# Filling expert buckets from both ends, and loading an expert's weights and a row block earlier, in a fused attention and mixture-of-experts kernel

## The chip, the cores and the metric

The kernel runs on one core of one Trainium2 chip. The metric is the device time of one execution in microseconds (us). Executions of one kernel on one chip mostly agree within about 1.5% (run 6 below spreads by 2.3%). The same kernel on different chips does not: the kernel before took about 524 us on two of the chips used here, and about 547 us on the chip of run 12 and on that of the first timed runs (the record gives no number for the latter; it may be the same chip). Every comparison below is between runs on the same chip.

## The reference, cut to what matters

Attention over 8 batches, 8 heads, 576 positions, head size 64, causal by blocks of 64. Its output, 4608 tokens of 512 numbers, goes through a router that picks two of eight experts for each token, and each expert is a two-layer network.

```python
logits = x @ w_gate
noisy_logits = logits + np.log1p(np.exp(x @ w_noise)) * noise
top2 = np.argpartition(-noisy_logits, 2, axis=1)[:, :2]
...                                   # softmax over the two: top2_w
for e in range(8):
    for k in range(2):
        mask = top2[:, k] == e
        h = np.maximum(x[mask] @ w1[e], 0.0)              # 512 -> 1024
        out[mask] += top2_w[mask, k, None] * (h @ w2[e])  # 1024 -> 512
```

## The kernel before

Attention runs in four groups of nine row tiles (128 tokens each). After each group a router on VectorE finds each token's two experts and its two slots, and 18 indirect transfers scatter the rows into `xd`, a buffer in device memory with eight buckets of `CAP` = 640 rows for each half of the tokens. The second half of the kernel works on 16 blocks, each one expert for one half: four experts of half 0, the same four of half 1, then experts 4 to 7 in turn for both halves.

A block's rows come by a transposing load from the SyncE queue (SP). Weights come by the GpSimd queue. A token's two experts are added by way of memory: the lower-numbered expert stores its weighted result to `yd` (`ysb`), the higher-numbered one gathers it (`yg`), adds it (`yo`) and scatters the sum to the output. Before the change a bucket mixes both kinds of rows, so every tile of experts 1 to 6 does both.

```python
def load_x(b):                                   # SP: one transposing load
    half, e = SEQ[b]
    xg = ffn["x"].tile([P, DB, CAP], BF16, tag="xg", name="xg")   # two buffers
    ins = nc.sync.dma_start_transpose(out=xg, in_=xd[half][e * CAP:(e + 1) * CAP, 0:Dm])
    for nm in scat[half]:                        # waits for all scatters of its half
        tc.add_manual_dep(ins.ins, nm, SYNC_DEP, reason="rows landed")
    xgs[b] = xg

def load_w(pool, e):                             # GpSimd: w1, then w2
    ...

def layer2(b, c):
    ...                                          # eight matmuls into yp
    if e + 1 < E:
        ysb = ffn["y"].tile([P, Dm], BF16, tag="ysb", bufs=4)
        nc.scalar.activation(out=ysb, in_=yp, func=AF.Copy, scale=w)
        nc.sync.dma_start(out=yd[half][e * CAP + c * P:e * CAP + (c + 1) * P, :], in_=ysb)
    if e:
        yo = ffn["y"].tile([P, Dm], F32, tag="yo", bufs=4)
        nc.vector.scalar_tensor_tensor(out=yo, in0=yp, scalar=w, in1=ygs.pop((b, c)),
                                       op0=ALU.mult, op1=ALU.add)
        ins = nc.gpsimd.indirect_dma_start(out=out, ...)          # by trow
```

The loop over the steps of the second half issues the loads. `at(slot, ...)` runs a job at the end of the same step.

```python
for b in range(NB):
    steps += [(layer1, b, fb) for fb in range(0 if b == 0 else 1, FB)]
    if b + 1 < NB:
        steps.append((layer1, b + 1, 0))
    steps += [(layer2, b, c) for c in range(CT)]
...
for fn, b, j in steps:
    fn(b, j)
    if fn is layer1 and j == FB - 1:
        if b + 2 < NB:
            if b + 2 == 4:
                at(slot, load_rec, 1)
                at(slot + 12, read_rec, 1)
            at(slot, load_x, b + 2)
        if b in (3, 7):
            at(slot, load_w, wL, 4 + (b - 3) // 4)
        if b in (5, 9):
            at(slot, load_w, wE, 6 + (b - 5) // 4)
    if fn is layer1 and SEQ[b][1] and j in GJ:
        gather(b, GJ.index(j))
    run(slot)
```

The softmax here doesn't subtract the row's maximum and nothing guards it: scores larger than these inputs give would overflow.

Of the kernel before, what the change touches and what calls it, by code (L numbers as in the profile page):

```python
# [8 lines left out]
F32 = mybir.dt.float32  # L9
BF16 = mybir.dt.bfloat16  # L10
# [9 lines left out]
def kernel(  # L20
# [23 lines left out]
    TG = 9  # L44
# [11 lines left out]
    ZR = 512  # L56
# [49 lines left out]
    qk_pool = right.enter_context(tc.tile_pool(name="qk", bufs=1, side="right"))  # L106
# [9 lines left out]
    ecend = consts.tile([P, E, 1], F32)  # L116
    ecap_i = consts.tile([P, E, 1], I32)
    rmask = consts.tile([P, E, TG], F32)
    ovrow_i = consts.tile([P, 2, TH], I32)
    ovrow = consts.tile([P, 2, TH], F32)  # L120
    base = [consts.tile([P, E, 1], F32, name=f"base{i}") for i in range(NH)]
# [11 lines left out]
    def setup_consts():  # L133
        nc.vector.memset(ones_mat, 1.0)
        nc.vector.memset(rmask, 1.0)
        nc.vector.memset(rmask[:, :, 0:1], 0.0)
# [23 lines left out]
        for i in range(NH):  # L160
            nc.vector.tensor_copy(base[i], ecap_i)
        nc.vector.tensor_copy(ebeg, ecap_i)
        nc.vector.tensor_scalar(ecend, ecap_i, float(CAP), None, op0=ALU.add)
# [9 lines left out]
    qT = qk_pool.tile([P, 73 * 64], BF16)  # L173
    kT = qk_pool.tile([P, 73 * 64], BF16)
    anchors = {}
    pace = {}
# [75 lines left out]
    def score_unit(g, u):  # L252
# [32 lines left out]
        pace["last"] = ins.ins.name  # L285
# [52 lines left out]
    def router(g):  # L338
        half, t0 = g // 2, g * TG
        lg = av_ps.tile([P, TG, 2 * E], F32, tag="av")  # L340
        for idx in range(TG):
            for db in range(DB):
# [26 lines left out]
        m = rt.tile([P, E, TG], BF16, tag="m")  # L369
        nc.vector.tensor_add(m, oh[:, 0], oh[:, 1])  # L370
# [4 lines left out]
        mf = m.rearrange("p e t -> p (e t)")  # L375
        pp = av_ps.tile([P, 2, E * TG], F32, tag="av")
# [3 lines left out]
        incl = rt.tile([P, E, TG], F32, tag="incl")  # L380
        nc.vector.tensor_tensor_scan(out=incl.rearrange("p e t -> p (e t)"),
                                     data0=rmask.rearrange("p e t -> p (e t)"),
                                     data1=pp[:, 0, :], initial=0.0, op0=ALU.mult, op1=ALU.add)
        pos = rt.tile([P, E, TG], F32, tag="pos")
        nc.vector.tensor_tensor(out=pos.rearrange("p e t -> p (e t)"),
                                in0=incl.rearrange("p e t -> p (e t)"), in1=pp[:, 1, :], op=ALU.add)
        yield
        nc.vector.tensor_tensor(out=pos, in0=pos, in1=base[half].to_broadcast([P, E, TG]), op=ALU.add)
        nc.vector.tensor_tensor(out=base[half], in0=base[half], in1=incl[:, :, TG - 1:TG], op=ALU.add)
        yield  # L390
        ov = rt.tile([P, E, TG], F32, tag="ov")
        nc.vector.tensor_tensor(out=ov, in0=pos, in1=ecend.to_broadcast([P, E, TG]), op=ALU.is_ge)
        nc.vector.scalar_tensor_tensor(out=pos, in0=ov, scalar=BIG, in1=pos, op0=ALU.mult, op1=ALU.add)
        yield
        sl2 = rt.tile([P, 2, TG], F32, tag="sl2")
        pk = rt.tile([P, 2, E, TG], F32, tag="pk")
        nc.vector.tensor_tensor(out=pk, in0=oh, in1=pos.unsqueeze(1).to_broadcast([P, 2, E, TG]),
# [30 lines left out]
    def scatter(g, j):  # L428
# [7 lines left out]
        tc.add_manual_dep(ins.ins, pace["last"], SYNC_DEP, reason="spreads the descriptors over time")  # L436
# [27 lines left out]
    def read_rec(half):  # L464
# [22 lines left out]
        nc.vector.tensor_tensor(out=fill, in0=rowid, in1=base[half].to_broadcast([P, E, CT]), op=ALU.is_lt)  # L487
# [10 lines left out]
    def layer1(b, fb):  # L498
        half, e = SEQ[b]
        w1sb = wload[e][0]  # L500
        if fb == 0:
            hs[b] = ffn["h"].tile([P, FB, CAP], BF16, tag="hsb", name="hsb")
# [8 lines left out]
        pace["last"] = ins.ins.name  # L511

    def layer2(b, c):
# [11 lines left out]
        if e:  # L525
# [14 lines left out]
    def gather(b, c):  # L540
# [10 lines left out]
        tc.add_manual_dep(ins.ins, pace["last"], SYNC_DEP, reason="spreads the descriptors over time")  # L551
# [23 lines left out]
    def clear_x(half, slot):  # L575

        for e in range(E):
            n = CAP - ZR
            ins = nc.sync.dma_start(out=xd[half][e * CAP + ZR:(e + 1) * CAP, :], in_=zero[0:n, 0:DR])
            after(ins, slot)  # L580
# [8 lines left out]
    def flags():  # L589
        nc.vector.tensor_tensor(out=fl, in0=base[0], in1=ecend, op=ALU.subtract)  # L590
        nc.vector.tensor_tensor(out=fl2, in0=base[1], in1=ecend, op=ALU.subtract)
        nc.vector.tensor_tensor(out=fl, in0=fl, in1=fl2, op=ALU.max)
        nc.vector.reduce_max(flm, fl[:, :, 0], axis=AX.X)
        nc.vector.tensor_scalar(flag_i, flm, 0.0, None, op0=ALU.is_gt)
# [4 lines left out]
    fl = keep.tile([P, E, 1], F32)  # L599
    fl2 = keep.tile([P, E, 1], F32)  # L600
# [67 lines left out]
    at(2 * UG + 22, load_w, wE, 0)  # L668
    at(3 * UG + 12, load_w, wE, 1)
    for u in range(NG * UG):  # L670
        score_unit(*divmod(u, UG))
        run(u)
        if u == 3 * UG + 18:
            raws_up.close()
            ffn["x"] = raws_up.enter_context(tc.tile_pool(name="xgp", bufs=2, side="right", reuse_waits="tile"))
            ffn["h"] = raws_up.enter_context(tc.tile_pool(name="hp", bufs=2, side="right", reuse_waits="tile"))
            load_x(0)
            load_rec(0)
            load_x(1)

# [13 lines left out]
    wL = None  # L694
    for fn, b, j in steps:
        fn(b, j)
        if fn is layer1 and j == FB - 1:
            if b + 2 < NB:
                if b + 2 == 4:
                    at(slot, load_rec, 1)  # L700
                    at(slot + 12, read_rec, 1)
                at(slot, load_x, b + 2)
            if b in (3, 7):
                at(slot, load_w, wL, 4 + (b - 3) // 4)
            if b in (5, 9):
                at(slot, load_w, wE, 6 + (b - 5) // 4)
        if fn is layer1 and SEQ[b][1] and j in GJ:
            gather(b, GJ.index(j))
        run(slot)
        slot += 1  # L710
        if slot == NG * UG + 6:
            top.close()
            wL = top.enter_context(tc.tile_pool(name="wL", bufs=3, reuse_waits="tile"))
# [92 lines left out]
```

## Time and profile before

| | us |
|---|---|
| timed runs, before the prediction (3) | 548.15 median, 546.17 to 548.84 |
| profiled run | 525.0, span 523.2 |
| granted TensorE clock in the profile | 0.885 |

The timed runs and the profile differ by 4.4%. The lines of the profile that carry the argument are shown and read in the prediction. In short: the expert stage is bound by TensorE (PE), with stretches in which PE stands idle, called holes here. Most of them lie in its first third, where weights, row loads and indirect transfers share the DMA engines. Two more words: a transfer is *issued* by an engine's queue (SP or GpSimd, in traces POOL) and *lands* when its last bytes have arrived.

### The profile page before, as it was taken

The page shows a single profiled execution, that of the slowest core. Times are in us where ns is not written, and L with a number is a line of the kernel's source. Part 1 is how long each engine was busy: PE and PEld are TensorE (multiplying, and loading weights), DVE is VectorE, ACT ScalarE, POOL GpSimd, SP SyncE. Part 2 cuts the span into 40 slices and gives each one's busy share as a digit, 9 for nine tenths or more (in the row PEclk, how much of TensorE's full clock was granted, in tenths as well). Part 3 has the DMA queues.
Part 4 walks back from the last instruction along what each step waited for, and adds up shares of the span by engine and source line. Part 5 has one row for each costly group of instructions (what it writes and reads, how often), then busy time and mean ns, then how long its engine had stood idle before and what let it go on. Part 6 is the DMA issues. An engine that isn't in the chain of part 4 may idle for free.

```text
span 523.2 us, 10093 instructions
## 1 busy us (share of the span) xinstructions
PE 424.6 (81%) x3944; PEld 257.6 (49%) x3944; DVE 182.5 (35%) x482; ACT 238.3 (46%) x319; POOL 294.5 (56%) x331
## 2 busy tenths in 40 slices
PE   2787978978871992596559999799699799999991
PEld 2455655745650751353235665465355455565550
DVE  4275797797880460020221102112122022112211
ACT  0856766767760240344114554454344434555230
POOL 9675285797571353387745225375276365565561
PEclk9957996998975896699669999999889989999997
DMA  8999799399779699661266929729939935645331
GB/s 133 146 145 214 110 183 208 116 127 187 186 145 187 92 170 221 161 163 66 67 144 129 233 64 193 165 79 201 196 116 186 239 123 169 156 145 183 122 103 50
DMA packets 142743, 78.77 MB, mean 151 GB/s; under 512 B 102931, under 2 KB 131754, under 8 KB 142688
## 3 DMA queue, kind: packets, MB, share of 16 engines
q0 software_dynamic: 73376, 55.87, 64.4%
q1 hardware_dynamic: 69312, 22.19, 20.8%
q8 instruction: 33, 0.54, 0.4%
q14 instruction: 22, 0.18, 0.1%
HBM read 71.43 MB, written 39.42 MB: 212 GB/s over the span
## 4 chain that ended last, share of the span: by engine, by line
PE 37%; DMA 18%; issue 16%; POOL 14%; DVE 6%; ACT 4%; SPq 2%; POOLq 1%; DVEq 0%; ACTq 0%
PE hp L506 14%; PE yp L518 13%; DMA yd<-ysb 7%; POOL out_dram L529 5%; POOL yg L547 4%; PE sc L266 3%; DMA xd<-xr,slots 3%; DMA t<-in_k_dram 3%; PE av L303 2%; ACT esc L269 2%; PE tp L228 2%; POOL xd L431 2%; DMA vt<-in_v_dram 2%; DMA t<-in_q_dram 2%; SPq L585 2%
## 5 line engine op out<-in xcount | busy, mean ns | idle before, releaser
L506 PE MATMUL hp<-xg,w1sb 128*128 128x320 bf16 x1024 | 149.5, 307 | 33.9 <-ACT hsb L509 22.3
L518 PE MATMUL yp<-w2sb,hsb 128*128 128x512 bf16 x640 | 149.0, 391 | 20.8 <-DVE yo L527 20.1
L527 DVE SCALAR_TENSOR_TENSOR yo<-yp,wrow,yg 128x512 f32<-128x512 f32 x70 | 52.5, 750 | 263.5 <-ACT ysb L523 155.3
L506 PEld LDWEIGHTS <-w1sb 128*128 128x128 bf16 x1024 | 102.3, 100 | 79.1 <-issue 34.8
L509 ACT ACTIVATE hsb<-hp 128x640 bf16<-128x640 f32 x128 | 89.8, 704 | 82.5 <-PE hp L506 82.5
L529 POOL DMA_INDIRECT out_dram<-yo,trow x70 | 69.6, 994 | 87.2 <-DVE yo L527 62.9
L269 ACT ACTIVATE esc<-sc 128x1024 bf16<-128x1024 f32 x96 | 94.4, 1029 | 52.1 <-PE sc L266 49.8
L518 PEld LDWEIGHTS <-hsb 128*128 128x128 bf16 x640 | 64.0, 100 | 100.4 <-issue 34.1
L523 ACT ACTIVATE ysb<-yp,wrow 128x512 bf16<-128x512 f32 x70 | 48.1, 687 | 127.9 <-PE yp L518 96.9
L431 POOL DMA_INDIRECT xd<-xr,slots x72 | 71.6, 994 | 58.0 <-ACT hsb L509 29.5
L547 POOL DMA_INDIRECT yg<-yd,orow x70 | 71.0, 1014 | 38.6 <-ACT hsb L509 22.1
L266 PE MATMUL sc<-qT,kT 64*128 64x512 bf16 (+4 forms) x320 | 43.8, 340 | 9.3 <-ACT esc L269 7.9
L195 POOL DMA_DIRECT2D vt<-in_v_dram x40 | 33.7, 879 | 14.7 <-PE av L314 10.0
L303 PE MATMUL av<-vt,esc 128*128 128x65 bf16 x640 | 35.6, 212 | 5.5 <-DVE xr L318 5.1
L303 PEld LDWEIGHTS <-esc 128*128 128x128 bf16 x640 | 27.9, 109 | 18.3 <-DVE xr L318 8.9
L228 PE MATMUL tp<-ident,t 128*64 128x128 bf16 x512 | 26.8, 268 | 6.1 <-DVE qT L233 3.7
L318 DVE TENSOR_TENSOR xr<-av,rden 128x256 bf16<-128x256 f32 x72 | 30.5, 424 | 2.6
L228 PEld LDWEIGHTS <-t 128*64 128x64 bf16 x512 | 21.5, 139 | 14.1 <-issue 6.2
L235 DVE COPY kT<-tp 128x1024 bf16<-128x1024 bf16 (+1 forms) x24 | 25.0, 1042 | 4.7 <-PE tp L228 4.2
L317 DVE RECIPROCAL rden<-av 128x4 f32<-128x4 f32 x72 | 13.0, 181 | 27.8 <-PE av L303 18.9
L266 PEld LDWEIGHTS <-kT 64*128 64x128 bf16 x320 | 11.5, 97 | 18.7 <-issue 11.7
L233 DVE COPY qT<-tp 128x1024 bf16<-128x1024 bf16 (+1 forms) x24 | 14.7, 612 | 16.7 <-PE tp L228 16.5
(110 smaller groups left out, 193.3 us busy)
## 6 DMA issues: line engine op xcount, KB each, us to landing
yd<-ysb SPq DMA_DIRECT2D x70, 128.0 KB
w1sb<-in_moe_w_dram POOLq DMA_DIRECT2D x8, 1024.0 KB
w2sb<-in_moe_w_dram POOLq DMA_DIRECT2D x8, 1024.0 KB
t<-in_q_dram POOLq DMA_DIRECT2D x16, 256.0 KB
t<-in_k_dram POOLq DMA_DIRECT2D x16, 256.0 KB
vt<-in_v_dram POOLq DMA_DIRECT2D x32, 128.0 KB
xd<-zero SPq DMA_DIRECT2D x16, 132.0 KB
nz_all<-in_moe_noise_dram SPq DMA_DIRECT2D x72, 2.0 KB
```

The lines of the kernel that those rows point to most:

```text
L228: nc.tensor.transpose(to[64 * hf:64 * hf + 64, :, r, :], raw[:, hf, r * 64:(r + 1) * 64], ident)
L266: nc.tensor.matmul(out=sc[:, hf, off:off + z - a], lhsT=kT[sl, c0 + jt * P:c0 + jt * P + P], rhs=qT[sl, c0 + a:c0 + z], start=True, stop=True)
L269: ins = nc.scalar.activation(out=esc[:, hh, :, piece * 512:(piece + 1) * 512], in_=sc, func=AF.Exp, scale=scale)
L303: nc.tensor.matmul(out=av[:, hh, :], lhsT=esc[:, hh, hf, c:c + P], rhs=vb[:, 4 * hf + jt, h, :], start=(jt == 0), stop=(jt == ib))
L431: ins = nc.gpsimd.indirect_dma_start(out=xd[half].bitcast(I32), out_offset=bass.IndirectOffsetOnAxis(ap=slots[:, g * TG + idx, i:i + 1], a ...
L506: nc.tensor.matmul(out=hp[:, n, 0:NW], lhsT=w1sb[:, db, fb * P:(fb + 1) * P], rhs=xgs[b][:, db, n * NW:(n + 1) * NW], start=(db == 0), sto ...
L509: ins = nc.scalar.activation(out=hs[b][:, fb, :].rearrange("p (n w) -> p n w", n=2), in_=hp[:, :, 0:NW], func=AF.Relu)
L518: nc.tensor.matmul(out=yp, lhsT=hs[b][:, fb, c * P:(c + 1) * P], rhs=w2sb[:, fb, :], start=(fb == 0), stop=(fb == FB - 1))
L523: nc.scalar.activation(out=ysb, in_=yp, func=AF.Copy, scale=w)
L527: nc.vector.scalar_tensor_tensor(out=yo, in0=yp, scalar=w, in1=ygs.pop((b, c)), op0=ALU.mult, op1=ALU.add)
L529: ins = nc.gpsimd.indirect_dma_start(out=out, out_offset=bass.IndirectOffsetOnAxis(ap=trow[half][:, e, c:c + 1], axis=0), in_=yo, in_offse ...
L547: ins = nc.gpsimd.indirect_dma_start(out=yg, out_offset=None, in_=yd[half][0:e * CAP, :], in_offset=bass.IndirectOffsetOnAxis(ap=orows[hal ...
```

## The change

It has two parts, and they serve one aim, which is to empty the holes.

**Buckets.** Rows whose expert is the token's first (lower-numbered) one fill their bucket from the top; rows whose expert is the second fill it from the bottom. Then only the lower row tiles of a bucket, `LT` of them, gather and write the output: 46 of each in place of 70. The router pays for it with seven more VectorE instructions for each group and doubled sizes of some others.

**Loads.** The weights of expert 2 and row block 2 come in the last attention group. Row loads move forward by some steps. The weights of experts 4 to 7 get new places: those of expert 5 move forward by four steps, those of experts 4, 6 and 7 back by one and a half to three and a half blocks. Now three of the four stand at step 3. Queries, keys and the hidden rows of layer 1 share one tile, `hq`.

```diff
+    LT = (0, 1, 2, 3, 3, 4, 5, 5)
...
+        c2 = rt.tile([P, TG, E], F32, tag="c2")          # running count in a token's row
+        nc.vector.tensor_tensor_scan(out=c2.rearrange("p t e -> p (t e)"), ...)
+        ms = rt.tile([P, 2, E, TG], BF16, tag="ms")      # [0]: minus first expert, [1]: second
+        nc.vector.scalar_tensor_tensor(out=msv[1], in0=c2, scalar=2.0, in1=m, op0=ALU.is_equal, op1=ALU.mult)
+        nc.vector.tensor_tensor(out=msv[0], in0=msv[1], in1=m, op=ALU.subtract)
... (positions, limits and choice of slot for both ends)
-        if e:
+        if c < LT[e]:
             yo = ffn["y"].tile([P, Dm], F32, tag="yo", bufs=4)
...
-    at(2 * UG + 22, load_w, wE, 0)
-    at(3 * UG + 12, load_w, wE, 1)
+    at(2 * UG + 24, load_w, wE, 0)
+    at(3 * UG + 15, load_w, wE, 1)
...
-            ffn["x"] = raws_up.enter_context(tc.tile_pool(name="xgp", bufs=2, ...))
+            ffn["x"] = raws_up.enter_context(tc.tile_pool(name="xgp", bufs=3, ...))
+            wM = raws_up.enter_context(tc.tile_pool(name="wM", bufs=1, ...))
             load_x(0)
             load_rec(0)
             load_x(1)
+            load_x(2)
+            load_w(wM, 2)
...
-        if fn is layer1 and j == FB - 1:
-            ... (row load b + 2, then weights, as above)
+        if fn is layer1:
+            if j == 0 and b and b + 2 < NB and b + 2 != 4:
+                load_x(b + 2)
+            if (b, j) == (3, 4):
+                load_rec(1)
+                load_x(4)
+            if (b, j) == (4, 3):
+                read_rec(1)
+            if (b, j) in WL:
+                load_w(*WL[b, j])
+            if j in GJ and GJ.index(j) < LT[SEQ[b][1]]:
+                gather(b, GJ.index(j))
...
+            WL = {(5, 7): (wE, 4), (7, 3): (wE, 5), (9, 3): (wM, 6), (11, 3): (wL, 7)}
```

Indirect transfers also wait for the activation before the last now (`pace[-2]`), not the last. The middle of each bucket, where valid rows may be missing, is cleared in 16 pieces of 96 rows for each half in place of eight of 128.

## The prediction

> **What bounds the kernel now.** I read the slices of the page first, for where TensorE (PE) is not busy, then the costliest groups, for what a block of the second half costs, then the chain of waits and the timeline, for what each hole waited for.
>
> The slices of the page, each 13.08 us of the 523.2:
>
> ```profile
> PE   2787978978871992596559999799699799999991
> DVE  4275797797880460020221102112122022112211
> PEclk9957996998975896699669999999889989999997
> ```
>
> Attention ends near 157 us, in slice 12 (counted from 0), where PE falls to 1. The expert stage runs from there. It is at 9 nearly throughout once past 270 us, but slices 15, 16, 18, 19 and 20 show 2, 5, 6, 5, 5. So the second half is bound by PE, with large holes in its first third. DVE matters in attention only.
>
> From the costliest groups: duration sums, mean ns of one, idle before:
>
> ```profile
> L506 PE MATMUL hp<-xg,w1sb 128*128 128x320 bf16 x1024 | 149.5, 307 | 33.9 <-ACT hsb L509 22.3
> L518 PE MATMUL yp<-w2sb,hsb 128*128 128x512 bf16 x640 | 149.0, 391 | 20.8 <-DVE yo L527 20.1
> L529 POOL DMA_INDIRECT out_dram<-yo,trow x70 | 69.6, 994 | 87.2 <-DVE yo L527 62.9
> L547 POOL DMA_INDIRECT yg<-yd,orow x70 | 71.0, 1014 | 38.6 <-ACT hsb L509 22.1
> ```
>
> 16 blocks (one expert of one half of the tokens) each have 64 matmuls of layer 1 and 40 of layer 2. In the chain, undisturbed, layer 1 of a block takes 8.69 us and layer 2 8.72 us: 17.4 us a block, 278.6 us for 16. PE really ends at about 511.7, 342.3 us after the stage starts at 169.4. About 11 us of that are the rest of the last attention group and its router. So some 52 us are holes and the slow clock after them. That is what can be won here.
>
> The chain of waits, start and duration in us, around the change of stage and in the first block:
>
> ```profile
> 151.20 12.51 DMA xd<-xr,slots
> 163.83 5.52 DMA xg<-xd
> 169.39 2.29 PE hp L506 x8
> ...
> 199.10 1.19 SPq L450
> 200.39 13.07 DMA yd<-ysb
> 213.57 0.70 ACT ysb L523
> ```
>
> The timeline has the holes themselves; the bracket is idle time and releaser:
>
> ```profile
> 186.29 14.01 SPq L450 DMA_TRANSPOSE xg<-xd  x1
> ...
> 214.90 8.37 PE L506 MATMUL hp<-xg,w1sb 128*128 128x320 bf16 x48 [15.81 <-ACT hsb L509]
> ...
> 222.22 2.50 SPq L450 DMA_TRANSPOSE xg<-xd  x1
> ...
> 253.82 8.05 PE L518 MATMUL yp<-w2sb,hsb 128*128 128x512 bf16 x24 [9.68 <-DVE yo L527]
> ...
> 270.39 9.61 PE L506 MATMUL hp<-xg,w1sb 128*128 128x320 bf16 x48 [6.35 <-ACT hsb L509]
> ```
>
> Hole A, 157.9 to 169.4: the last scatter of half 0 takes 12.5 us to land, because expert 1's weights were issued just ahead of it (147.68 and 148.48); then the first transposing load takes 5.5. Hole B, 15.8 us: the load of row block 2 needs 14.01 us to issue on the SP queue beside the weights of expert 2 (from 182.3); the ysb stores stand behind it in that queue and need 13 us more beside expert 3's weights; there are four ysb buffers, so the fifth ysb of block 0 waits, and ScalarE (ACT) with it. Hole C, 9.7 us: GpSimd (POOL) issues an indirect transfer every 1.3 us from about 229 to 258 (18 scatters of the last group, gathers and output scatters in between); the gather for yo comes late. Hole D, 6.35 us: row block 4 waits for the last half-1 scatter (issued 257.1), and again stores stand behind the transpose. Hole E, 2.8 to 3.0 us each or in pairs near 339, 374, 379 and 418, 10.6 in sum: the fifth yo waits for a buffer whose output scatter is behind a weight load, so POOL is late with the next gathers.
>
> **What the Trainium skill says.** "DMA: Bandwidth & Descriptors", section "Queues, rings and completion order": each DMA engine takes the rows it has work for in turn, a packet at a time, and data of one ring is consumed in ring order. The trace agrees: a scatter behind weights took 12.5 us against 2.46 for one with none before it (at 239.63), and a transpose from SP beside weights took 14.01 us against 2.50. The same page, "Issuing engines are not separate DMA queues", says that all queues share 16 engines; so moving the weights earlier only moves the contention. "TensorE: Matmul & The Clock Gate", section "Part 1: The HAM clock gate", has the clock fall to half after an idle of about 3.4 us. The trace agrees: after hole C 24 matmuls took 8.05 us, 335 ns each, against 218.
>
> **The change part by part.** (1) Rows whose expert is the token's first are filled from the top, the others from the bottom; only bottom tiles gather and write the output. The limits (0,1,2,3,3,4,5,5) add to 23, so 46 gathers and 46 output scatters replace 70 of each. 48 POOL issues of 1.3 us go: 62 us of POOL, none directly on PE's path but in C and E. 24 DVE yo of 0.75 us go as well (18 us, DVE idle there). The valid rows moved stay the same. I counted the reference's routing for this draw: at most 361 rows for the 384 of expert 4, 416 of 512 for expert 5, 580 of 640, and 624 of 640 in a bucket, so the slow fallback is not taken.
>
> Between 200 and 262 blocks 1 to 3 need 2, 4 and 6 indirect transfers in place of 10 each: 18 x 1.3 = 23 us less POOL beside the 18 remaining scatters. C should vanish: 9.7 us, and 2.8 of slow clock (24 x (335-218) ns): 12.5. E should mostly go: blocks of experts 4 and 5 have 3 and 4 yo tiles for four buffers, and the last weights are issued in block 11, before those of five tiles. 10.6 plus 3 of clock, less 3 that I leave: 10.6.
>
> (2) Loads. Expert 2's weights and row block 2 now come in the last attention group; one expert instead of two is loaded from block 0 on. In A, expert 1's weights follow the last scatter. It is issued at 151.2 - 1.2 (it now waits for the activation before the last) - 1.8 (two weight issues no longer ahead) + 4.5 (DVE, below) = 152.7 and lands 3 us later, 155.7, not 163.7. But the transpose now runs beside 8.4 MB of weights, at 14 to 15 us as at 186.29, not 5.5: rows come at about 170.5. So A is a wash, +1. In B, SP has four transposes in a row beside weights; experts 1 to 3 (12.6 MB at about 270 GB/s, 8.4 MB in the 31 us from 182.3 to 213.6) end near 202 rather than 214. The first stores then go at about 205 and land 3 us later. PE resumes at 209 instead of 214.9: 6 us won.
>
> (3) Row block 4 and the records of half 1 are issued in block 3, at layer 1 step 4, only four steps (4 x 1.09 = 4.4 us) before they are needed; records (about 3 us, from 5.44 against 2.5 for the transpose behind them at 260.24) and load (5.5) take 8.5. D becomes a wait of 4 us plus 1.5 of clock in place of 6.35 plus 3.1: 4 us won.
>
> (4) The router has seven more DVE instructions and larger ones. By its own rows: a scan 0.29, three strided writes (0.28 more for one, 0.48 for two; line 360's is 0.48), one more comparison 0.23, three for the choice 0.69, doubled sizes 0.3: 2.8 us a group. In attention DVE is at 12.0 of 13 us in the stretch from 65 to 78, so I let 80% of three groups count: 6 us later at the end of attention, 4.5 of it ahead of half 0's last scatter (in A already). The fourth runs under the experts. Clearing 16 pieces in place of 8 per half adds SP issues of 0.6 us that nothing waits for.
>
> **Sum.** PE resumes after B at 209. From there 117 steps of layer 1 (1.088) and 75 of layer 2 (1.744) remain: 258 us. Add 5.5 for row block 4, 2 for a late half-1 scatter (the next load waits for it on SP), 3 for what stays of E: 477.5. The tail behind the last matmul (511.7 to 523.2, 11.5) stays: 489. The timed runs are longer than the profiled one by 548.15/523.2; 489 x 1.0477 = 512.
>
> **The rivals.** First, A gets worse: the first transpose shares the engines with two experts' weights throughout, and takes longer than 14 us since 18 scatters of group 2 are in the rings too. For it: the 14.01. Against: at 186.29 there were six scatters as well. If the start slips 8 us and B does not shrink, 489 becomes 503, or 527 timed. Second, the SP queue is the bound in B: four transposes at 14 us from 155.7 end at 212, and B stays whole, only C to E are won: 495, 519 timed. Third, better than I think: transposes are as quick as 5.5 us, so PE starts when attention does end, at 164, and B vanishes (resuming at 195): 475, 498 timed. For it: the transpose at 369.48 took 5.45 with a weight load nearly done. Fourth, the fill is hidden: if C to E only reappear as one later POOL wait, the time stays within 2%; against it, from 425 to 500 PE runs without holes with all ten indirect transfers a block, so POOL keeps up where scatters and weights are absent.
>
> **Range and chances.** C and E (23 us) rest on counts, so under 2% (537) needs both to fail. I predict 512 us, 498 to 529 with 8 in 10; faster by over 2% 0.92, within 2% 0.06, slower 0.02.
>
> **What would show it.** Right: 46 of lines 529 and 547; no PE wait of 9 us on yo; the last half-0 scatter lands 3 us after its issue; the first transpose takes 14 us and PE starts near 170; a short wait for row block 4; PE at clock 1.0 from about 240; routers longer by 2.8 us of DVE. Wrong: a hole over 8 us before the first layer 1, SP waits of 10 us or more from block 1 on, or attention ending later than 166.

## The result, and the profile after

| chip | kernel before | changed kernel | ratio (95% interval) |
|---|---|---|---|
| first, "547" | 547.16 (544.61 to 548.84, 4 runs) | 565.88 (560.91 to 567.79, 4 runs) | 1.033 (1.025 to 1.041) |
| second, "524" | 524.46 (521.7 to 529.16, 7 runs) | 540.79 (538.54 to 542.93, 4 runs) | 1.031 (1.023 to 1.039) |

Times are medians in us, and the result is correct. A ratio here and below is the mean time of one kernel's fast runs over that of the other's fast runs of the same rounds, so not quite the ratio of the medians. The changed kernel is 3% slower on both kinds of chip, where 6.6% faster was predicted.

The profiles compared below are both from the second chip: the kernel before run again (span 526.3 us, 3 us more than the profile that the prediction used) and the changed kernel run again (span 536.6 us). First the busy slices of PE, of the kernel before (13.2 us each) and of the changed kernel (13.4 us each):

```profile
PE   2787978888781991695649999799699799999991
```

```profile
PE   2795968967975199799599969949968996999990
```

The weak slices of the kernel before, 15 to 20 (1, 6, 9, 5, 6, 4), are nearly gone: the middle is fuller, and the weakest slice there is a 5. But further on there are now a 6, a 4, a 6 and a 6 (slices 23, 26, 29 and 33, from 308 us to 456), where the kernel before had 7, 6 and 7. The groups confirm the counts: 46 gathers and 46 output scatters, at the durations known.

```profile
L556 POOL DMA_INDIRECT out_dram<-yo,trow x46 | 45.8, 995 | 104.1 <-DVE yo L554 100.9
L574 POOL DMA_INDIRECT yg<-yd,orow x46 | 47.3, 1027 | 79.8 <-ACT hq L536 41.4
```

The chain of waits has the first new loss:

```profile
160.54 25.11 DMA xg<-xd
```

The first row load took 25.11 us to land, against 5.52 in the prediction's profile. The timeline of the same stretch shows what it ran beside. (The columns are start, duration, engine, line, operation, tiles, count; "SPq" is the issue on SP's queue.)

```profile
158.70 0.83 POOL L212 DMA_DIRECT2D w1sb<-in_moe_w_dram  x1
...
160.44 0.78 POOL L212 DMA_DIRECT2D w1sb<-in_moe_w_dram  x1
160.54 9.13 SPq L478 DMA_TRANSPOSE xg<-xd  x1
...
185.69 2.29 PE L533 MATMUL hp<-xg,w1sb 128*128 128x320 bf16 x8 [15.53 <-DMA xg<-xd]
```

Two experts' weights are issued just ahead of it, and PE waits 15.5 us. The clock falls with it, as the Trainium skill, "TensorE: Matmul & The Clock Gate", section "Part 1: The HAM clock gate", says of idle stretches: the granted clock is 0.50 in the 2.4 us from 185.6, and the first eight matmuls of layer 1 take 2.29 us where eight at clock 1.0 take 1.25 (from 192.28). To see how the loss goes on, I cut the span at the same pieces of work in both kernels, read from the timelines (the first layer-1 activation of block 0, and the last layer-1 activation of later blocks). "Predicted" is the prediction's own term.

| stretch | before, us | after, us | difference | predicted |
|---|---|---|---|---|
| start to first layer 1 | 173.1 | 188.0 | +14.9 | +1 (hole A) |
| to end of block 1 | 49.2 | 39.2 | -10.0 | -7 (hole B, after that +1) |
| to end of block 5 | 91.7 | 77.7 | -14.0 | -12.5 (C) and -4 (D) |
| to end of block 15 | 192.1 | 208.9 | +16.8 | -10.6 (E) |
| to end of span | 20.2 | 22.8 | +2.6 | 0 |
| sum | 526.3 | 536.6 | +10.3 | |

So the middle of the expert stage, to block 5, was won about as predicted, and two rows are wrong: the start and, above all, blocks 6 to 15. There the block of 17.4 us would give 174 us for ten of them; before took 192, after 209. The timeline of the changed kernel around block 6:

```profile
301.80 0.85 POOL L212 DMA_DIRECT2D w1sb<-in_moe_w_dram  x1
...
304.91 10.70 SPq L478 DMA_TRANSPOSE xg<-xd  x1
315.70 6.04 SPq L551 DMA_DIRECT2D yd<-ysb  x5
320.71 0.69 ACT L550 ACTIVATE ysb<-yp,wrow 128x512 bf16<-128x512 f32 x1 [7.02 <-DMA yd<-ysb]
322.05 9.13 PE L533 MATMUL hp<-xg,w1sb 128*128 128x320 bf16 x48 [5.22 <-ACT hq L536]
```

And the same meeting in the kernel before, where the weights of expert 4 are issued:

```profile
279.20 2.52 SPq L450 DMA_TRANSPOSE xg<-xd  x1
281.39 0.85 POOL L202 DMA_DIRECT2D w1sb<-in_moe_w_dram  x1
...
289.76 0.69 ACT L523 ACTIVATE ysb<-yp,wrow 128x512 bf16<-128x512 f32 x1 [1.78 <-DMA yd<-ysb]
```

Before, the row load went first and needed 2.52 us on SP; the weights came 2.2 us later. After, the weights go first and the row load needs 10.70 us. The stores of `ysb` stand behind it on SP, the fifth `ysb` finds all four buffers taken, ScalarE waits 7.0 us and PE 5.2. The slow row load repeats at 347, 392 and 436 (11.0, 9.9 and 9.5 us), but there PE waits for something else. The chain of waits:

```profile
347.34 13.30 DMA yg<-yd,orow
360.74 0.76 DVE yo L554
361.55 5.11 PE yp L545 x16
```

At 347.34 a gather is issued, just behind the weights (344.76 and 346.12) on GpSimd's queue. It lands after 13.30 us, where two gathers in the chain of the kernel before took 2.58 and 3.19, and `yo` and PE wait for it. At 389.31 and 433.08 the same happens (14.49 and 13.54 us). So the new place of the weights makes holes on two paths: stores behind a slow row load (the first hole), and gathers behind the weights themselves (the other three). From 300 us on the changed kernel has four PE waits over 5 us (5.2, 7.8, 6.7 and 5.8, together 25.5); before has four from 2.0 to 3.3 (together 10.8). The theory that I took into the experiments saw only the first path: *the new place of the weights of experts 4 to 7, ahead of the row loads, costs some 16 us; the first row load beside two experts' weights costs the rest; the buckets are worth what was predicted.* The rivals were that the buckets themselves cost the time (a dearer router, other transfers), and that the row loads are long wherever they stand.

### The profile page after: what moved, and what is told of

Read it like the earlier page. It is cut to its first block, busy times and chain, and to the rows that moved or that the text cites.

```text
span 564.4 us, 9944 instructions
## 1 busy us (share of the span) xinstructions
PE 446.0 (79%) x3944; PEld 268.1 (48%) x3944; DVE 175.5 (31%) x490; ACT 238.9 (42%) x319; POOL 247.2 (44%) x291
## 3 DMA queue, kind: packets, MB, share of 16 engines
q0 software_dynamic: 70304, 55.78, 59.6%
HBM read 68.28 MB, written 34.21 MB: 182 GB/s over the span
## 4 chain that ended last, share of the span: by engine, by line
PE 46%; DMA 17%; issue 14%; POOL 9%; DVE 7%; ACT 3%; another core or an unknown queue 1%; POOLq 0%; SPq 0%; DVEq 0%; ACTq 0%
PE hp L533 16%; PE yp L545 15%; DMA xg<-xd 6%; PE sc L276 4%; POOL yg L574 4%; POOL out_dram L556 3%; PE av L313 3%; PE tp L238 2%; DMA yg<-yd,orow 2%; PE av L324 2%; DMA t<-in_q_dram 2%; PE tp L342 2%; DMA t<-in_k_dram 2%; DMA vt<-in_v_dram 2%; DMA out_dram<-yo,trow 1%
## 5 line engine op out<-in xcount | busy, mean ns | idle before, releaser
L545 PE MATMUL yp<-w2sb,hq 128*128 128x512 bf16 x640 | 150.5, 393 | 25.5 <-DVE yo L554 21.5
L536 ACT ACTIVATE hq<-hp 128x640 bf16<-128x640 f32 x128 | 89.6, 704 | 88.7 <-PE hp L533 81.1
L554 DVE SCALAR_TENSOR_TENSOR yo<-yp,wrow,yg 128x512 f32<-128x512 f32 x46 | 34.3, 750 | 283.5 <-ACT ysb L550 200.1
L545 PEld LDWEIGHTS <-hq 128*128 128x128 bf16 x640 | 64.0, 100 | 106.6 <-issue 37.9
L556 POOL DMA_INDIRECT out_dram<-yo,trow x46 | 45.8, 996 | 110.7 <-DVE yo L554 107.3
L574 POOL DMA_INDIRECT yg<-yd,orow x46 | 47.2, 1027 | 81.9 <-ACT hq L536 54.5
L276 PE MATMUL sc<-hq 64*128 64x512 bf16 (+4 forms) x320 | 48.4, 372 | 11.5 <-ACT esc L279 9.9
L313 PEld LDWEIGHTS <-esc 128*128 128x128 bf16 x640 | 30.5, 114 | 23.7 <-DVE xr L328 10.6
L205 POOL DMA_DIRECT2D vt<-in_v_dram x40 | 33.8, 876 | 14.7 <-PE av L324 10.6
L245 DVE COPY hq<-tp 128x1024 bf16<-128x1024 bf16 (+1 forms) x24 | 25.0, 1042 | 6.3 <-PE tp L238 3.7
L324 PE MATMUL av<-vt,esc 128*64 128x65 bf16 (+1 forms) x320 | 17.2, 226 | 10.9 <-issue 6.3
L276 PEld LDWEIGHTS <-hq 64*128 64x128 bf16 x320 | 12.5, 100 | 21.7 <-issue 14.4
```

Of the source, the lines that this page charges most:

```text
L276: nc.tensor.matmul(out=sc[:, hf, off:off + z - a], lhsT=kT[sl, c0 + jt * P:c0 + jt * P + P], rhs=qT[sl, c0 + a:c0 + z], start=True, stop=True)
L313: nc.tensor.matmul(out=av[:, hh, :], lhsT=esc[:, hh, hf, c:c + P], rhs=vb[:, 4 * hf + jt, h, :], start=(jt == 0), stop=(jt == ib))
L536: ins = nc.scalar.activation(out=hs[b][:, fb, :].rearrange("p (n w) -> p n w", n=2), in_=hp[:, :, 0:NW], func=AF.Relu)
L545: nc.tensor.matmul(out=yp, lhsT=hs[b][:, fb, c * P:(c + 1) * P], rhs=w2sb[:, fb, :], start=(fb == 0), stop=(fb == FB - 1))
L556: ins = nc.gpsimd.indirect_dma_start(out=out, out_offset=bass.IndirectOffsetOnAxis(ap=trow[half][:, e, c:c + 1], axis=0), in_=yo, in_offse ...
L574: ins = nc.gpsimd.indirect_dma_start(out=yg, out_offset=None, in_=yd[half][0:e * CAP, :], in_offset=bass.IndirectOffsetOnAxis(ap=orows[hal ...
```

## The experiments

Each run has the kernel before timed on the same chip in the same rounds. All twelve gave correct results, and all but the last ran on "524" chips (two of them).

**1. The kernel before again.** No edit; it gives the profile that is the base above.

> The kernel before, profiled a second time. Its first profile ran 525 us, but its timed runs 545 to 549, so one of the two may not be typical. If the first profile was a lucky one, this one runs about 546 us with attention ending 10 to 20 us later than 157 us and the clock at half for longer; if the timed runs lose their 22 us elsewhere, this profile shows 525 again.

Measured: 528.09 us against 524.37, ratio 1.007 over two runs. The first profile was typical of this kind of chip, and the difference to 547 us is one of chips, not of profiling. It also shows how far a ratio can be trusted: the same kernel, timed under two labels, differs from itself by 0.7%, with an interval (1.003 to 1.010) that leaves 1 out. Ratios within about 1% of 1 are read as "the same" below.

**2. The buckets alone.** The changed kernel with the load schedule, pools and pacing of before.

```diff
-            if j == 0 and b and b + 2 < NB and b + 2 != 4:
-                load_x(b + 2)
-            ... (the new load schedule)
+        if fn is layer1 and j == FB - 1:
+            if b + 2 < NB:
+                ...
+                at(slot, load_x, b + 2)
+            if b in (3, 7):
+                at(slot, load_w, wL, 4 + (b - 3) // 4)
```

> Only the bucket part of the change (router, limits, 46 gathers and scatters, clearing); the loads as before. Theory 1, the loads cost the time and the buckets save it: 515 to 530 us, no 9 us wait on yo, experts starting within 6 us of where before starts them. Theory 2, the longer router costs it (attention later by 15 us or more in the third and fourth group): 545 us or more, with the first layer 1 at 185 us or later.

Measured: 532.38 us (529.93 to 533.82), ratio 1.013 (1.009 to 1.017). 24 gathers and 24 scatters fewer, and the kernel is 1.3% slower, with the very schedule of before. The timeline of this kernel where expert 4's weights come:

```profile
268.91 0.85 POOL L210 DMA_DIRECT2D w1sb<-in_moe_w_dram  x1
269.09 11.49 SPq L476 DMA_TRANSPOSE xg<-xd  x1
...
288.32 8.56 PE L532 MATMUL hp<-xg,w1sb 128*128 128x320 bf16 x48 [7.27 <-ACT hsb L535]
```

The program order is that of before, row load first. But GpSimd no longer has a backlog of gathers and scatters, so it issues the weights 0.2 us ahead of the row load, not 2.2 behind. The backlog had kept the two apart by accident. The other three meetings are alike (10.2, 11.6 and 13.1 us of issue), and all four holes are on the path of the stores (7.3, 4.7, 10.9 and 7.5 us): here the weights still stand behind the gathers. This is the part that I had not thought of at all. Two other things of this trace: attention ends 14 us later than in the kernel before, of which run 7 explains some 9.6, and the last matmul ends 9.9 us later, though the span is only 5.6 us longer (see "The tail" below).

**3. The loads alone.** The kernel before with the new load schedule (and the pacing and the tile `hq` that go with it) and 70 gathers and scatters.

```diff
+            load_x(2)
+            load_w(wM, 2)
...
+            if j == 0 and b and b + 2 < NB and b + 2 != 4:
+                load_x(b + 2)
...
+            WL = {(5, 7): (wE, 4), (7, 3): (wE, 5), (9, 3): (wM, 6), (11, 3): (wL, 7)}
```

> Only the load part (expert 2's weights and row block 2 in the last attention group, one tile for q, k and h, later weights four steps ahead of a row load, pacing on the activation before the last); router, 70 gathers and 70 scatters as before. Theory 1: slower than the changed kernel or like it, 560 to 580 us, first transpose landing 20 us or more after its issue. Theory 2: near before or faster, 530 to 550, first layer 1 at 170 to 175.

Measured: 542.39 us (538.51 to 545.02), ratio 1.031 (1.025 to 1.038). The loads alone cost as much as the whole change, and the buckets alone cost 1.3%. The parts don't add up: each suffices to bring weights and row loads together (three row loads need 10.7 to 11.6 us here). The three holes there, of 7.1 to 8.2 us, end on gathers issued behind the weights, which take 11.2 to 14.4 us to land.

**4. The weights written behind the row load.** In the changed kernel the four weight loads are put right behind the row load in the program.

```diff
-            WL = {(5, 7): (wE, 4), (7, 3): (wE, 5), (9, 3): (wM, 6), (11, 3): (wL, 7)}
+            WL = {(6, 0): (wE, 4), (8, 0): (wE, 5), (10, 0): (wM, 6), (12, 0): (wL, 7)}
```

> The changed kernel, with the weights of experts 4 to 7 issued right behind a row load (block 6, 8, 10, 12, step 0) rather than four or eight steps ahead of one. If the weights ahead of the transposes cause the holes at 338, 370, 416 and 461 us (5.4 + 13.6 + 7.9 + 12 us in the chain), these go: 530 to 545 us, and each of those transposes issues in 2.5 to 3.5 us, not 10. If the holes come from gathers that wait for the stores of the block before, whatever the transposes do, they stay and the time is within 1% of the changed kernel's 566.

Measured: 544.77 us (543.76 to 548.46), ratio 1.041 (1.036 to 1.045). A miss, and a useful one. The timeline:

```profile
302.57 0.85 POOL L212 DMA_DIRECT2D w1sb<-in_moe_w_dram  x1
...
305.70 10.73 SPq L478 DMA_TRANSPOSE xg<-xd  x1
```

The weights are still issued 3.1 us ahead. The row load on SP waits until layer 1 has read the block whose buffer it takes; GpSimd waits for nothing. The experiment never made the condition that it was to test. An order of two queues has to be made with a dependency. But it separates the two paths: the weights now stand behind the gathers, no gather takes over 3.7 us from issue to landing, and all four holes (5.6, 7.1, 6.8 and 9.6 us) come from stores behind a slow row load. That path alone is enough for the whole loss.

**5. The changed kernel again.** No edit; its numbers are in the result above.

> The changed kernel unaltered, so that it can be compared on the same chip as the other runs: its first runs were beside a kernel before of 547 us, the last four kernels beside one of 524. If chips only scale, 524 x 1.033 = 541 us; if the first chip hit it harder in attention, below 540.

**6. The weights behind the row load by a dependency.** The four weight loads wait for the second `ysb` activation of the block, so the row load is well ahead.

```diff
-            WL = {(5, 7): (wE, 4), (7, 3): (wE, 5), (9, 3): (wM, 6), (11, 3): (wL, 7)}
+            WL = {(5, 1): (wE, 4), (7, 1): (wE, 5), (9, 1): (wM, 6), (11, 1): (wL, 7)}
...
+        elif (b, j) in WL:                       # after layer2(b, 1)
+            load_w(*WL[b, j], dep=lasty[0])
```

> The changed kernel, with the weights of experts 4 to 7 made to wait for the second ysb of layer 2 in blocks 5, 7, 9 and 11, so that they start some 4 us behind a row load rather than ahead of it. In the last try they stood behind the row load in program order only, and GpSimd, which waits for nothing there, still issued them 1 to 3 us ahead. Theory: a row load that meets weights needs 10 to 13 us to issue, the stores behind it come late, and PE stands 5 to 10 us at the fifth ysb. Then here each row load issues in 2.5 to 4 us, the four holes (5.6, 7.1, 6.8, 9.6 us before) shrink to under 2 each, and the time is 20 to 30 us under the changed kernel's on this chip. Rival, stores are slowed by the weights themselves: holes stay at 4 us or more, and the time falls by under 8 us.

Measured: 524.75 us (519.19 to 531.16; one of the four is slow, and the median of the others is 522.75), ratio 0.996 (0.984 to 1.008), so 16 to 18 us less than the changed kernel's 540.79 in the same rounds. The profile puts it where it was looked for: block 5 ends at 305.1 in both, and blocks 6 to 15 take 193.2 us in place of 208.9. The timeline:

```profile
305.08 2.56 SPq L480 DMA_TRANSPOSE xg<-xd  x1
310.71 0.84 POOL L212 DMA_DIRECT2D w1sb<-in_moe_w_dram  x1
...
331.01 4.43 PE L547 MATMUL yp<-w2sb,hq 128*128 128x512 bf16 x10 [4.05 <-DVE yo L557]
```

The same row load takes 2.56 us. The edit also puts the weights of experts 5 to 7 behind the gathers of their block, so it clears both paths at once. What is left is a wait of `yo` of 3 to 4 us in each of the four places, where the next gathers run beside the weights (one issued at 322.58 takes 7.53 us to land).

**7. A dearer router alone.** The kernel before with ten idle VectorE instructions for each group, of the sizes that the change adds.

```diff
+        nc.vector.tensor_tensor_scan(out=dm..., data1=m..., initial=0.0, op0=ALU.mult, op1=ALU.add)
+        for _ in range(2):
+            nc.vector.tensor_tensor(out=db_.rearrange("p e t -> p t e"), in0=dm, in1=dm, op=ALU.add)
+        extra(dm, 1)                             # and 2 and 4 more in later steps
```

> The kernel before, with 10 idle VectorE instructions on a spare tile in each group's router, 2.8 us by the durations of such instructions, nothing else. If the later attention of the bucket part (14 us at its end) is VectorE time, attention ends 10 to 15 us later here too, though three routers add only 8.5 us, with more time at half clock; the first layer 1 moves by less, since it waits for the rows (+0 to +8 us). If it is the clearing or another wait of the bucket part, attention ends at most 5 us later.

Measured: 526.95 us, ratio 1.003 (0.996 to 1.011). Attention ends about 9.6 us later (its last exponential starts at 166.2 instead of 156.7), a little more than the 8.6 us that the added instructions of three groups take (2.9 a group), yet the total stays: the delay is taken up by the wait for rows and by later slack. In the changed kernel the same point is at 166.0, 9.4 us later than before. So added VectorE work of this size is enough to explain the later end of attention in the changed kernel (not all of the 14 us of run 2), and in the kernel before it costs no time.

**8. The mirror.** The kernel before with its weights of experts 4 to 7 moved ahead, from the end of layer 1 to its fourth step, and nothing else.

```diff
+        if fn is layer1 and j == 3:
             if b in (3, 7):
-                at(slot, load_w, wL, 4 + (b - 3) // 4)
+                load_w(wL, 4 + (b - 3) // 4)
```

> The kernel before, with the weights of experts 4 to 7 issued at step 3 of the same layer 1 instead of after step 7; the mirror of after_w_behind. If a row load that meets weights is the cause of the later holes, four row loads take 10 us or more here, holes of 5 us or more appear at the ysb behind them, and the time rises by 10 to 25 us. Rival: the 70 gathers and scatters on GpSimd keep the weights behind the row loads anyway, or the stores catch up: within 1% of before.

Measured: 549.22 us (547.1 to 550.19), ratio 1.047 (1.040 to 1.053), 25 us more than before (19 between the two profiles). The four row loads need 10.1 to 11.4 us. One of them:

```profile
318.87 0.86 POOL L202 DMA_DIRECT2D w1sb<-in_moe_w_dram  x1
322.02 10.27 SPq L450 DMA_TRANSPOSE xg<-xd  x1
...
335.63 4.69 PE L518 MATMUL yp<-w2sb,hsb 128*128 128x512 bf16 x12 [7.34 <-DVE yo L527]
```

The size was expected, the place of the holes was not: none is at `ysb`. All four (6.8 to 8.0 us) end on a gather that was issued behind the weights and took 11.2 to 12.0 us to land, for the edit moves the weights ahead of the gathers too. With 6 and 8 it is shown from both sides that the place of the weights causes the loss in blocks 6 to 15: mending it in the changed kernel wins 16 us, putting it into the kernel before loses 25. Which of the two paths the loss takes they don't separate; run 4 does, and run 10. The rival that row loads are long wherever they stand falls.

**9. The first stage.** Expert 1's weights go early in the last attention group, expert 2's behind the second step of layer 1.

```diff
-    at(3 * UG + 15, load_w, wE, 1)
+    at(3 * UG + 1, load_w, wE, 1)
...
-            load_w(wM, 2)
...
+            if (b, j) == (0, 1):
+                load_w(wM, 2, dep=pace[-1])
```

> The changed kernel with only the loads around its first row load altered: expert 1's weights fourteen units earlier in the last attention group, expert 2's only behind the second step of the first layer 1. In the changed kernel the first row load was issued at 160.5 us beside 8.4 MB of weights and landed at 185.7; attention had ended by 168. Both theories expect the first layer 1 at 168 to 175 instead of 188. Theory A, that wait costs time by itself: the end of block 1 moves with it, from 227 to 212 to 218, and the total by 10 us or more. Theory B, the stage is bound by the bytes (12.6 MB of weights wherever they stand): the wait comes back at the fifth ysb of block 0, block 1 still ends at 223 to 229, and the total moves by under 5 us.

Measured: 529.81 us (528.0 to 532.5), ratio 1.008, where the changed kernel has 1.031. The first row load needs 2.79 us of issue in place of 9.13, and the first layer-1 activation moves from 188.0 to 181.7, less than expected, because the last scatters of half 0 now stand behind expert 1's weights and the load is issued at 173.2. Block 1 ends at 227.6, as before the edit (227.2): an 11.5 us wait at the fifth `ysb` came back in block 0. So in the profile the gain of the first stage is given back by block 1, as the second theory expected of block 1. Its PE work even ends at 522.9 us, the changed kernel's at 522.4, while the timed runs say 11 us. The spans of the two profiles differ by 6.1 us (530.5 against 536.6), and all of that lies behind the last matmul: GpSimd's closing drain takes 1.13 us in place of 7.01 (see "The tail" below). So the earlier first row load is not shown to win anything; the rest of the 11 us lies between two chips and two sets of rounds, and the profiled execution (532.5) is the slowest of its four.

**10. Row loads later.** The row loads go at the fourth step of layer 1 instead of the first; row block 4 and the second half's records are exchanged.

```diff
-            if j == 0 and b and b + 2 < NB and b + 2 != 4:
+            if j == 3 and b and b + 2 < NB and b + 2 != 4:
                 load_x(b + 2)
-            if (b, j) == (3, 4):
-                load_rec(1)
+                if b == 3:
+                    load_rec(1)
+            if (b, j) == (3, 0):
                 load_x(4)
```

> The changed kernel with each row load three steps later (step 3 of layer 1 rather than step 0, so after the stores of layer 2 before it have been issued), and row block 4 three or four steps earlier, with row block 5 behind it; weights where the change has them. If the holes come from stores that stand behind a slow row load in SP's queue, they go although two or three of the row loads still meet weights and take 7 us or more: no hole over 4 us between block 4 and block 15, 15 to 25 us under the changed kernel (1.031 of before), so 0.98 to 1.00 of before. If it is the slow row load itself, or weights beside the stores, four holes of 4 us or more stay and the time falls by under 8 us.

Measured: 521.71 us (516.12 to 523.89; without the slow one 516.12 to 523.75), ratio 0.990 (0.982 to 0.998). The profiled execution was slow, so only the pattern of its trace is used:

```profile
326.28 2.80 SPq L478 DMA_TRANSPOSE xg<-xd  x1
330.08 0.85 POOL L212 DMA_DIRECT2D w1sb<-in_moe_w_dram  x1
332.67 1.08 POOL L574 DMA_INDIRECT yg<-yd,orow  x1 [0.30 <-ACT hq L536]
...
347.22 3.15 PE L545 MATMUL yp<-w2sb,hq 128*128 128x512 bf16 x7 [8.23 <-DVE yo L554]
```

All row loads from block 2 on need 2.4 to 3.5 us, the waits at `ysb` are gone, and so is the wait for row block 4. But the expected "no hole over 4 us" failed: three holes of 8.2, 5.8 and 5.5 us stay, at the places where the changed kernel has 7.8, 6.7 and 5.8. The gather is issued 2.6 us behind the first of the weights on the same queue and takes 13.66 us to land, and `yo` waits for it. So these three holes of the changed kernel are not made by the slow row loads: with quick ones they stay. So weights need a place behind the row load *and* behind the gathers.

**11. All of it together.** The edits of 9 and 10; the weights of experts 4 to 7 behind the last gather of blocks 5, 7, 9 and 11, with a dependency on that step's activation; and the router's tiles `m` and `ms` written contiguously, read strided by the matmul.

```diff
-            WL = {(5, 7): (wE, 4), (7, 3): (wE, 5), (9, 3): (wM, 6), (11, 3): (wL, 7)}
+            WL = {(5, 7): (wE, 4), (7, 7): (wE, 5), (9, 7): (wM, 6), (11, 7): (wL, 7)}
...
             if j in GJ and GJ.index(j) < LT[SEQ[b][1]]:
                 gather(b, GJ.index(j))
+            if (b, j) in WL:
+                load_w(*WL[b, j], dep=pace[-1])
...
-        nc.vector.tensor_add(m.rearrange("p t e -> p e t"), oh[:, 0], oh[:, 1])
+        nc.vector.tensor_add(m, ohv[0], ohv[1])
-        ms = rt.tile([P, 2, E, TG], BF16, tag="ms")
+        ms = rt.tile([P, 2, TG, E], BF16, tag="ms")
```

> All that the runs point to, together: buckets from both ends; expert 1's weights early and expert 2's behind the first layer 1; row loads behind the stores; weights of experts 4 to 7 behind the last gather of blocks 5, 7, 9, 11; and the router's new tiles written in the order in which VectorE passes them (three strided 0.48 us writes become 0.25). Sum of the single gains against the changed kernel: 16 to 20 us for the later holes, 5 for row block 4, 0 to 12 for the first stage, 2 for the router: 500 to 512 us where before takes 524. If the gains give way to one another, as the ones of the change did, 515 or more.

Measured: 493.18 us (491.63 to 496.69), ratio 0.938 (0.933 to 0.943), better than expected and faster than both kernels. Its slices (12.4 us each) and one meeting:

```profile
PE   2768797888799769959879999999899999999980
```

```profile
333.54 0.81 POOL L212 DMA_DIRECT2D w1sb<-in_moe_w_dram  x1 [3.44 <-ACT hq L538]
341.77 10.13 SPq L480 DMA_TRANSPOSE xg<-xd  x1
...
354.55 5.38 PE L547 MATMUL yp<-w2sb,hq 128*128 128x512 bf16 x24 [1.84 <-DVE yo L556]
```

PE is at 9 from slice 21 to slice 37, but for one 8. Cut at the same places as above, blocks 6 to 15 take 176.3 us, 32.6 less than in the changed kernel and close to the 174 of ten undisturbed blocks; block 1 ends 14.9 us earlier, and the stretch from there to block 5 is 5.7 us longer. The row load of the next block but one still meets the weights and needs 10.13 us, a gather issued at 342.65 needs 10.97, and PE loses only 1.8 us. So a slow row load or gather is not harmful in itself. It was harmful where a store or a gather that PE needed soon stood behind it or behind the weights. Several edits went in together here, so what each is worth in this kernel is not shown.

**12. The combined loads with the old buckets.** To see whether the loads alone make the gain.

```diff
-        if c < LT[e]:
+        if e:
...
-            if j in GJ and GJ.index(j) < LT[SEQ[b][1]]:
+            if SEQ[b][1] and j in GJ:
                 gather(b, GJ.index(j))
```

(and the router of before; the edit is shown against the kernel of 11)

> The combined kernel's loads (and pacing, and one tile for q, k and h) with the buckets, the router and the 70 gathers and 70 output scatters of the kernel before: what are the two-ended buckets worth once the loads are placed well? By the holes of before that go with them (9.7 us with the slow clock behind it near 254, about 3 us behind each later weight load) 10 to 25 us, less the 9 us by which the old router ends attention earlier where nothing else holds the stage up: 500 to 515 us, that is 0.955 to 0.98 of before against 0.938. Rival: the loads were everything, and the old buckets now run as fast, 0.93 to 0.945.

Measured, on a "547" chip: 548.41 us (547.06 to 554.22) against 547.32, ratio 1.004 (0.997 to 1.012). A miss: I expected the loads to be worth 2 to 4.5% alone. Here they are worth nothing without the buckets. PE waits 12.1 us at 260.5 and 7.4 at 273.2 for `yo`, whose gathers stand in GpSimd's backlog, and five more times for about 3 us. The quotient of the two ratios, 0.938/1.004 = 0.934, is what the new buckets and the router's layout bring once the loads are in place. It is taken across two kinds of chip, so its last digit means little.

| | old loads | loads of the change | loads of run 11 |
|---|---|---|---|
| old buckets | 1 | 1.031 | 1.004 |
| new buckets | 1.013 | 1.031 | 0.938 |

## Why the prediction was wrong, point by point

**Holes C and D: right.** From block 1 to the end of block 5 the prediction takes 12.5 and 4 us away; 14.0 went. It goes with the buckets: with the loads alone (run 3) the same stretch takes 93.4 us, with neither 91.7. There are 46 issues each and no 9.7 us wait for `yo` any more. Row block 4's wait was put at 4 us and measured 4.76.

**Hole E: the step that failed.** The prediction wrote: "E should mostly go: blocks of experts 4 and 5 have 3 and 4 yo tiles for four buffers, and the last weights are issued in block 11, before those of five tiles." It took off 10.6 us; blocks 6 to 15 took 16.8 us more, a miss of 27 us. The step counted `yo` buffers and gathers, and did not work out where the moved weight loads land against the row loads on SP and against the gathers on GpSimd's own queue. The diff has it: weights at step 7 of block 5 and step 3 of blocks 7, 9 and 11, and the next row load at step 0 of the following block, one or five steps of 1.09 us later, with the weights still under way; and at step 3 the gathers of that step and the next ones stand behind them. The prediction had the cost of such meetings in hand, 14.01 us against 2.50 for a row load and 12.5 against 2.46 for an indirect transfer behind weights, and used it only for the first blocks. In the changed kernel one hole (5.2 us) came from the row load, three (20.3 us) from gathers of 13.3 to 14.5 us. Run 6 puts a number on the place of the weights: 15.7 us of this stretch. The other 11 us of the miss are the gain that was counted and did not come: run 6 still takes 193.2 us here, the kernel before 192.1. It came only in run 11 (176.3), where nothing that PE needs soon stands behind the weights or behind a slow row load. A second cause was out of sight: GpSimd's backlog, which the prediction counted as pure loss, kept weights behind row loads. Run 2 shows that taking the backlog away brings the meeting about without any move of a load.

**Hole A: a term too small.** "[T]he transpose now runs beside 8.4 MB of weights, at 14 to 15 us", rows at 170.5. It was issued at 160.5, not 155.7, and took 25.1, so they came at 185.7. The first rival ("the first transpose shares the engines with two experts' weights throughout, and takes longer than 14 us") described it, but put the slip at 8 us. It was 14.9.

**Hole B: about right.** The second rival ("four transposes at 14 us") put PE's resumption late. From the first layer 1 to the end of block 1 10.0 us were won, against 7 predicted, and the remaining idle time at the old place of hole B is 3.0 us.

**The router: cost about right, effect too small, but cheap.** 2.8 us a group were predicted and 2.45 measured (9.17 against 6.72 us of VectorE, means over the four groups). "6 us later at the end of attention" became 9.4. Run 7 reproduces that with idle instructions and shows that in the kernel before it costs nothing.

**The tail and the chips.** 11.5 us were taken over for the tail; it became 14.2. No run was made for it, but the packed traces have it: GpSimd's closing drain takes 4.64 us in all four traces of the kernel before and its small edits (twice unchanged, runs 7 and 8), 7.01 in the changed kernel, 1.13 in run 9 and 0.72 in run 2. What sets it no run shows, but it goes with the program and not with the wait that an edit was meant for, so a few us between two kernels can be this. The factor 548.15/523.2 was read as timed against profiled runs; it was most likely two chips. A ratio to each chip's own time would not have been hurt by that.

**The verdict on the third and fourth rival.** Neither described what happened. The fourth ("C to E only reappear as one later POOL wait") came nearest: three of the four new waits are for gathers on GpSimd's queue (late in landing, not in being issued), the other for stores behind SP's row load, and it was worse than a wash. The prediction's own signs of being wrong did show: a hole of 15.5 us before the first layer 1, row loads of 10 us and more on SP, and an attention that ends just after 166.

What stays open: on its first, "547" chip the changed kernel ended attention some 25 us later than on the "524" chip. Four PE pauses of 1.1 to 1.5 us that the trace lays to nothing it records are 4.8 us of that; the granted clock over attention (from 30 us) was 0.72 there against 0.82, and whether that is cause or effect no run shows. Open too are what sets the closing drain, and what run 9 gained besides.

## What to carry to other kernels

Work that looks like a mere burden on a queue can be what keeps two transfers apart. Before taking it away, look up where every load that it delayed will go, and what it will meet there. Make the order of loads on different queues with dependencies, and give large loads a place behind both the small loads that PE needs soon and the gathers on their own queue. And test the parts of a change together as well as alone: here each was a loss alone, and together, with the loads in new places, the gain was about the size that had been counted (6.2% against 6.6%), though not term by term.

## What the Trainium skill lacked or had wrong

- "DMA: Bandwidth & Descriptors", section "Rules for kernel authors", says that a transpose next to ordinary DMAs "needs nothing". It speaks of correctness there; what it lacks is the cost in time: beside weight loads the issue of a transposing load of 640 rows took 10 to 13 us in place of 2.5, and its landing 25.1 us beside two experts' weights in place of 5.5.
- The same page, section "Queues, rings and completion order", does not say that an issuing queue is held for as long as a slow transpose is being issued. Here stores written behind it started at 315.70, just after the 10.70 us from 304.91.
- The same page, section "Latency and other measured facts", gives 261 GB/s as the effective rate of transposes, for one access pattern. One of 655 KB (128 x 4 x 640 numbers of two bytes) took 5.5 us from issue to landing here, so 119 GB/s with its fixed part; beside two experts' weights it was 26 GB/s.
- No page that I read says what an indirect transfer's out-of-bounds rows cost. With 24 gathers and 24 scatters fewer, and the same number of valid rows, the profile's counters fell from 71.43 to 68.28 MB read and from 39.42 to 34.21 MB written. 3,072 rows of 1 KB are 3.15 MB; the same rows of 2 KB, less 1.1 MB for more clearing, are 5.2 MB. So the counters seem to take out-of-bounds rows as moved. The packet table of the same pages does not: GpSimd's queue moved 55.87 MB before and 55.78 after. This is arithmetic, not an experiment.
- No page that I read says that one kernel's time differs by chip: 524 against 547 us here, 4.4%.
